# Another issue order in a fused attention and expert kernel: squares are copied behind their masks, first outputs stand behind last copies

## The chip, the core and the metric

The kernel runs on one core of one Trainium2 chip. The metric is the device time of one launch in microseconds (us). The engines are named as in the profile: PE (TensorE), PEld (its weight loads), ACT (ScalarE), DVE (VectorE), POOL (GpSimd) and SP (SyncE, which issues most transfers). PSUM, the memory that PE writes, has eight banks here; ACT and DVE copy results out of it.

## What is computed

Three stages follow each other. The first is a linear attention with a complex decay, for 4 batches, 8 heads, 768 positions and a head dimension of 48:

```python
for t in range(S):
    new_re = ar * S_re - ai * S_im
    new_im = ar * S_im + ai * S_re
    S_re, S_im = new_re + k[t] (outer) v[t], new_im
    y[t] = q[t] @ S_re            # per batch and head
```

Its output, 3072 rows of 384, goes to eight experts (each row to one, by the largest gate, if `x @ w_skip > 0`): `out = x + gate * relu(x @ w1[e]) @ w2[e]`. The last stage is `max(x @ w1, x @ w2, x @ w3) @ w_out`.

## The kernel before

The kernel is one program in which a planner, the class `Plan`, writes down all operations with engine, estimated duration, what they read and write, and a bias; `order()` then plays them through with these estimates and issues the instructions in the order in which they start there. Each engine works through its own list in that order, and the program adds a semaphore wait wherever an instruction touches something that an earlier one, in the issue order, still uses. For a PSUM bank these waits are between any two engines that use the bank, readers included: where ACT's copy out of a bank is issued ahead of DVE's reading of it, DVE waits for ACT, and the other way round. The planner of before does not know all of these waits: its keys name parts of a bank.

A level orders what is ready on an engine: earlier operations first, shifted by the bias, which comes from the table `PRIO` (one number for each kind of operation and unit of work). On PE the planner adds `TURN = 95` ns where the tiling form of the matmuls changes (whole array, 128 rows by 64 columns, 64 by 64), and prefers an operation of the current form over others unless its level is more than `KEEP` behind.

The attention has two parts that run beside each other. The **front end** takes five units of work (batches 0, 1 and 2, and batch 3 in two pieces). On ACT (L443) and DVE (L475, L513, L559) it works out magnitudes, phases and running products of the decay from `wa`, `wCD`, `wR` and scales q and k (`wqk`); each unit needs two sets of ACT functions, so two table loads (L378). Transfers on SP (L570) then stack the result into `qks`. The **steps** are 48: 6 chunks of 128 positions for two halves of the heads and 4 batches. One step consists of

- L607 (PE, whole array): a transposition of k into a `pk` bank, copied by ACT at L609 to `kn`;
- L620 (PE): products of k and q, "squares", into one of two `pp` banks (bank_109 and bank_110). DVE multiplies four of the six by a mask at L623, and ACT copies the other two at L626, both into `pt`, of which there are two;
- L636 (PE): the running state in banks 113 and 114, copied by ACT at L641 to `st`;
- L651 (PE), not for the first chunk: the "first output", q times the state, into one of two `py` banks (bank_111 and bank_112);
- L658 (PE, 64 by 64): the squares times v and `cross`, added to the same columns of the same `py` bank; ACT copies the sum at L661 to `ysb`;
- L665 (PE): `ysb` times `w9p` into other columns (`px`) of the same bank; ACT takes these out with the "last copies", L673 to `xt` and L675 to `lgw`.

The step after the next uses the same `py` bank, so its L651 (or L658, in a first chunk) meets the last copies there. Behind the attention come the experts and the last stage, whose operations are all recorded at L49. Their first operations are mixed into the last steps.

Of the kernel before, what the change touches and what calls it, by code (L numbers as in the profile page):

```python
# [58 lines left out]
class Plan:  # L59
# [6 lines left out]
    BASE = ()  # L66
    YIELD = None
    TURN = 95
    KEEP = 10

    def __init__(self, flat=None):

# [63 lines left out]
    def order(self):  # L136
# [21 lines left out]
        while done < n:  # L158
# [4 lines left out]
            for e, q in ready.items():  # L163
                if q and free[e] <= now:
                    k = 0
                    if e == "PE":
                        k = min(range(len(q)), key=lambda k: q[k][0] + (self.form.get(q[k][1], 0) != last) * self.KEEP)
                    i = q[k][1]
# [35 lines left out]
    def issue(self):  # L204
        for i in self.order():
# [37 lines left out]
MERGE = dict(ratio=(1, 1, 1, 1, 3), log=(1, 1, 1, 2, 3), size=(1, 1, 1, 1, 1), inv=(1, 1, 1, 1, 1),  # L243
             newton=(1, 1, 1, 2, 1), angle=(1, 1, 1, 2, 2), turn=(1, 1, 1, 1, 2), trig=(1, 1, 1, 1, 3))
LATE = 1
PRIO = dict(FE=(-30, 400, 400, 100, 60), FT=(250, 400, 100, 300, 10), AE=(300, 60, 0, 150, 0), AT=(-200, 250, 10, 30, 0),
            scale=(0, 200, 10, -30, -30), fin=(60, 200, 200, 250, 30), kn=(250, -100, -30, -150), free=(-150, 400, 0, 250),
            mask=(200, 300, 250, 0), z=(-60, 60, -100, 60), ysb=(-200, 200, -100, -150), xt=(-150, -150, -150, -150))
NXT = 2
NCD = 3  # L250
NQK = 3
# [49 lines left out]
def attention(tc, ctx, pl, a4, qk4, v, vx, w9, x_dram, lg, ident, phend, rhoend, keep, banks, swap, shift):  # L301
# [61 lines left out]
    mask = const.tile([P, HC], F32, name="mask")  # L363
# [66 lines left out]
    def load_cross(b, c):  # L430

        if (b, c // VG) not in crosses:
            t, k = crosses[b, c // VG] = pl.take("cross")
            cols = slice(c // VG * VG * VW, (c // VG + 1) * VG * VW)
            pl.dma(lambda: nc.sync.dma_start(out=t[:, :VG * VW], in_=vx[b][:, cols]), 5 * P * VG * VW, (), (k,),
                   after=stacked.get(b - 1, ()))
        return crosses[b, c // VG]
# [3 lines left out]
    def A_(f, out, in_, **kw):  # L441
        act(t_act(out[0].free_size()) + (94 if not isinstance(kw.get("bias", 0.0), float) else 0),
            lambda: nc.scalar.activation(out=out[0], in_=in_[0], func=f, **kw), keys(in_), keys(out))  # L443
# [3 lines left out]
    def many(us, nm):  # L447

        if len(us) == 1:
            return T[us[0], nm]  # L450
        (tag, h), (b, g, c0, c1) = tags[nm], us[0]
        k, cf = homes[tag, b, g][1:]
        return wide[tag][:, k[1]:k[1] + len(us), h, C * (c0 - cf):C * (c1 - cf)], keys(*(T[u, nm] for u in us))
# [14 lines left out]
    def keys(*ts):  # L468
        return sum((t[1] for t in ts), ())

    def V_(name, out, *ins, n=None, bias=0, **kw):
        fn = getattr(nc.vector, name)
        t = (t_dcp if name == "tensor_scalar" else t_dve)(out[0].free_size() if n is None else n)
        names = ("in0", "in1")[:len(ins)]
        pl.add("DVE", t, lambda: fn(out=out[0], **{m: i[0] for m, i in zip(names, ins)}, **kw),  # L475
               keys(*ins), keys(out), bias=bias)
# [4 lines left out]
    def ratio(us):  # L481
# [4 lines left out]
        for w in runs(us, "a", "ratio"):  # L486
            A = many(w, "ar")
            A_(AF.Ln, many(w, "C"), A, scale=1.0 - TINY)
            A_(AF.Exp, many(w, "D"), many(w, "C"), scale=-1.0 - TINY)
            V_("tensor_tensor", many(w, "ai"), many(w, "D"), many(w, "ai"), op=ALU.mult, bias=PRIO["FE"][now[0]])  # L490

    def stage_e(us):
# [5 lines left out]
        for w in runs(us, "CD", "size"):  # L498
            Ct = many(w, "C")
            V_("scalar_tensor_tensor", Ct, many(w, "ar"), Ct, scalar=1.0 / 0.999, op0=ALU.mult, op1=ALU.max, bias=PRIO["FE"][now[0]])  # L500
            for u in w:
# [6 lines left out]
    def decay(u):  # L508
# [3 lines left out]
        def scan():  # L512
            nc.vector.tensor_tensor_scan(out=Dt[0], data0=Dt[0], data1=Ct[0],  # L513
                                         initial=rhoend[:, i:i + 1] if c0 else INV0, op0=ALU.mult, op1=ALU.mult)
        pl.add("DVE", t_scan(n), scan, keys(Ct, Dt) + (("rho", i),), keys(Dt), bias=PRIO["FE"][now[0]])
        pl.add("DVE", 75, lambda: nc.vector.tensor_copy(out=rhoend[:, i:i + 1], in_=Dt[0][:, n - 1:n]), keys(Dt), (("rho", i),),  # L516
               bias=PRIO["FE"][now[0]])

    def scale(us):
# [3 lines left out]
        for w in runs(us, "CD", "newton"):  # L523
            R0, Ct, Dt = many(w, "R0"), many(w, "C"), many(w, "D")
            V_("scalar_tensor_tensor", R0, Dt, Ct, scalar=-1.0, op0=ALU.mult, op1=ALU.mult, bias=PRIO["scale"][now[0]])
            V_("scalar_tensor_tensor", Ct, R0, Ct, scalar=2.0, op0=ALU.add, op1=ALU.mult, bias=PRIO["scale"][now[0]])
            for u in w:
# [48 lines left out]
    def qkeys(b, h, c):  # L576
        i = (2 * b + h // 4) % NST
        return tuple(("qks", i, h % 4, ri, e, c) for ri in range(2) for e in range(0, D, 16))
# [3 lines left out]
    def step(b, hh, c):  # L582
# [3 lines left out]
        hk = sum((qkeys(b, 4 * hh + h, c) for h in range(4)), (("blank", i),))  # L586
        vt, vk = T[b, "v"]
# [3 lines left out]
        xv, xk = load_cross(b, c)  # L591
# [9 lines left out]
        if not last:  # L601
            pk, pkk = pl.take("pk")
            kn, knk = pl.take("kn")
# [9 lines left out]
        pt, ptk = pl.take("pt")  # L613

        free = ("free", ptk)
        p6, t6 = six(pp), six(pt)

        def f():
            for j, n, o in heads:
# [3 lines left out]
        masked = pl.add("DVE", t_dve(4 * HC) + 10, lambda: nc.vector.tensor_tensor(  # L623
            out=t6[:, 0:4], in0=p6[:, 0:4], in1=mask[:, None, :].to_broadcast([P, 4, HC]), op=ALU.mult), (ppk,), (ptk,),
            bias=PRIO["mask"][b])
        pl.add("ACT", t_acp(2 * HC), lambda: nc.scalar.copy(pt[:, 4 * HC:6 * HC], pp[:, 4 * HC:6 * HC]), (ppk,), (free,),  # L626
               bias=PRIO["free"][b])
        sp = prev.get((b, hh)) if c else None
        if not last:
            z = zst[hh][:, 0:4 * ZW]  # L630
# [13 lines left out]
        py, pyk = pl.take("py")  # L644
        px = py[:, XO:XO + 2 * XW].rearrange("p (j w) -> p j w", j=2)
        py = py[:, 0:2 * C].rearrange("p (j t) -> p j t", j=2)
        ysb, ysk = pl.take("ysb")
# [3 lines left out]
                nc.tensor.matmul(py[side[h % 2], h // 2, :], sp[0][:, h * D:h * D + 64], Q[:, h, sl], start=h < 2, stop=False,  # L651
                                 skip_group_check=True)
        if c:
            pl.add("PE", 4 * 109, f, hk + (sp[1], ("px", pyk)), (pyk,), form=1)

        def f():
            for j, n, o in heads:
                nc.tensor.matmul(py[side[o], j, n * HC:], half(j, n, o), t6[side[o], quads(j, n), :],  # L658
                                 start=c == 0 and j + n == 0, stop=n == 1, skip_group_check=True)
        pl.tail = masked, pl.add("PE", 4 * 165, f, (vk, xk, ptk, free), (pyk,), form=2)  # L660
        pl.add("ACT", t_acp(256), lambda: nc.scalar.copy(ysb, py), (pyk,), (ysk,), bias=PRIO["ysb"][b])  # L661
        def f():
            for j in range(2):
# [5 lines left out]
        xt, xtk = xts[b, c]  # L669
# [20 lines left out]
    def steps(us):  # L690
        for b, g, c0, c1 in us:
            if (b, "v") not in T:
                load_v(b)
            done[b, g] = c1
        new = []
        for k, (b, hh) in enumerate((b, hh) for b in range(B) for hh in range(2)):
            c1 = min(done.get((b, g), 0) for g in (hh, hh + 1))
            c0 = stepped.get((b, hh), 0)
            new += [(c - c0, k, b, hh, c) for c in range(c0, c1)]
            stepped[b, hh] = c1  # L700
        for _, _, b, hh, c in sorted(new):
            step(b, hh, c)
# [1078 lines left out]
```

## Time and profile before

| | us |
|---|---|
| median of 3 runs | 681.35 (677.01 to 682.12) |
| profiled execution, its own time | 681.32 |
| profiled execution, span of its instructions | 679.6 |
| PE busy | 597.0 (88% of the span) |
| PEld busy | 550.7 (81%) |
| DVE busy | 457.3 (67%) |
| ACT busy | 384.6 (57%) |

The profiled execution is one run on the chip. An engine is busy while one of its instructions runs; for PE this is an upper reading, since matmuls overlap and their ends are modelled. Idle time is put down to the instruction whose semaphore came last. The shares are means over stages of very different make: PE does nothing before about 52 us, works on the steps until about 234 us, and then on the experts and the last stage.

### The profile page before, as it was taken

Reading aid. Unit: us, or ns where it says so; the run is one execution under the profiler, and the core shown is the slowest. Engines: PE = TensorE matmul, PEld = TensorE weight load, DVE = VectorE, ACT = ScalarE, POOL = GpSimd, SP = SyncE. Lnnn points to the kernel's source line nnn. Section 1 sums busy time; section 2 is a strip of 40 time slices with the busy share of each in tenths; the row PEclk is TensorE's granted clock in tenths of the full one; section 3 lists DMA queues with packets and bytes.
Section 4 is the critical chain, followed back from the end, with each engine's and each line's share of the span. In section 5 each row is a group of like instructions: output and inputs, shape, how many; then the busy total and the mean of one; then the engine's idle time right before and its main releaser. Section 6 shows DMA issues by size and latency. Waiting matters only on the chain.

```text
span 679.6 us, 14174 instructions
## 1 busy us (share of the span) xinstructions
PE 597.0 (88%) x5669; PEld 550.7 (81%) x5669; DVE 457.3 (67%) x748; ACT 384.6 (57%) x800; POOL 64.5 (9%) x73
## 2 busy tenths in 40 slices
PE   0008789979999999989999998999999999999996
PEld 0007678968888889979999997889899898998996
DVE  5998978969778775999999954845547365303120
ACT  7798979889875755776676532432324333213121
POOL 1000000000003130030200143404011000000000
PEclk9999999989999999999999999999999999999999
DMA  9979769797658767887786366315043050010000
GB/s 306 296 186 257 284 176 303 250 264 254 177 165 239 249 200 240 276 273 264 261 270 218 117 186 210 117 68 182 30 152 105 1 197 13 12 36 0 25 25 28
DMA packets 60025, 117.40 MB, mean 173 GB/s; under 512 B 6032, under 2 KB 45472, under 8 KB 59952
## 3 DMA queue, kind: packets, MB, share of 16 engines
q1 hardware_dynamic: 51584, 84.57, 40.1%
q10 hardware_dynamic: 4512, 19.66, 8.2%
q0 software_dynamic: 3856, 12.19, 6.1%
q8 instruction: 46, 0.75, 0.5%
q14 instruction: 27, 0.22, 0.1%
HBM read 82.59 MB, written 12.58 MB: 140 GB/s over the span
## 4 chain that ended last, share of the span: by engine, by line
PE 68%; ACT 10%; DVE 9%; DMA 7%; issue 3%; SPq 1%; POOL 0%; ACTq 0%; POOLq 0%; DVEq 0%
PE bank L49 56%; PE bank L658 3%; PE bank L620 3%; ACT wCD L443 3%; ACT wa L443 3%; PE bank L651 2%; DMA qks<-wqk 2%; PE bank L636 2%; PE bank L665 2%; DVE wqk L475 1%; DMA wraw<-y_slot,r_grow 1%; DVE u L49 1%; DMA wqk<-in_qk 1%; DMA x<-in_m 1%; DVE wa L559 1%
## 5 line engine op out<-in xcount | busy, mean ns | idle before, releaser
L49 PE MATMUL bank<-ar,wh 128*128 128x512 f32 (+1 forms) x504 | 137.1, 360 | 0.1
L49 PEld LDWEIGHTS bank<-ar,wh 128*128 128x128 f32 x504 | 90.0, 189 | 14.1 <-DVE xs L49 0.3
L49 PE MATMUL bank<-ar,wl 128*128 128x512 f32 (+1 forms) x252 | 90.6, 360 | 0.0
L49 DVE TENSOR_TENSOR xs<-bank,xs 128x512 f32<-128x512 f32 (+1 forms) x42 | 25.8, 614 | 69.3 <-PE bank L49 69.2
L607 PE MATMUL bank<-ident,qks 96*128 96x96 f32 x160 | 23.2, 272 | 52.3 <-DMA qks<-wqk 52.3
L49 PE MATMUL bank<-ar,sm 128*128 128x384 f32 x348 | 67.0, 338 | 0.0
L49 PE MATMUL bank<-xth,ar 128*128 128x256 f32 x312 | 63.5, 288 | 3.0 <-DVE sm L49 2.1
L607 PEld LDWEIGHTS bank<-ident,qks 96*128 96x128 f32 x160 | 15.7, 147 | 55.6 <-issue 46.7
L49 PEld LDWEIGHTS bank<-ar,sm 128*128 128x128 f32 x348 | 59.2, 189 | 0.0
L49 DVE TENSOR_TENSOR ar<-wraw,ar 128x768 fp32r<-128x768 f32 x58 | 54.7, 953 | 4.8 <-ACT ar L49 4.5
L49 PEld LDWEIGHTS bank<-xth,ar 128*128 128x128 f32 x312 | 50.9, 190 | 5.0 <-DVE sm L49 3.4
L49 PE MATMUL bank<-woh,sm 128*128 128x384 f32 x192 | 53.9, 334 | 0.0
L49 ACT CAST ar<-wraw 128x768 fp32r<-128x768 f32 x58 | 48.1, 835 | 9.8 <-PE bank L49 8.6
L49 PEld LDWEIGHTS bank<-ar,wl 128*128 128x128 f32 x252 | 47.6, 189 | 7.1
L49 ACT COPY ysb<-bank 128x384 f32<-128x384 f32 x40 | 18.4, 478 | 60.8 <-PE bank L49 60.6
L443 ACT ACTIVATE wCD<-wCD 128x768 f32<-128x768 f32 (+3 forms) x67 | 51.4, 785 | 2.3 <-DVE wCD L513 2.1
L658 PE MATMUL bank<-pt,v 64*64 64x64 f32 (+1 forms) x384 | 42.3, 253 | 3.2 <-ACT xt L673 1.4
L620 PE MATMUL bank<-qks 128*64 128x128 f32 (+1 forms) x768 | 44.1, 260 | 0.7 <-DVE rhoend L516 0.5
L49 PE MATMUL bank<-xtl,ar 128*128 128x256 f32 x156 | 44.0, 282 | 0.0
L49 ACT ACTIVATE wraw<-wraw 128x768 f32<-128x768 f32 x24 | 19.6, 842 | 42.4 <-DVE u L49 36.6
L658 PEld LDWEIGHTS bank<-pt,v 64*64 64x64 f32 x384 | 36.2, 136 | 8.8 <-ACT xt L673 2.6
L443 ACT ACTIVATE wa<-wa 128x768 f32<-128x768 int32 (+8 forms) x53 | 40.9, 792 | 3.8 <-DVE wa L559 3.2
(223 smaller groups left out, 1422.1 us busy)
## 6 DMA issues: line engine op xcount, KB each, us to landing
wraw<-in_w SPq DMA_DIRECT2D x62, 384.0 KB, 4.5
wraw<-in_a ACTq DMA_DIRECT2D x12, 768.0 KB, 5.2
wqk<-in_qk SPq DMA_DIRECT2D x9, 768.0 KB, 10.0
x<-in_m ACTq DMA_DIRECT2D x9, 768.0 KB, 6.3
qks<-wR SPq DMA_DIRECT2D x18, 288.0 KB, 4.6
qks<-wqk SPq DMA_DIRECT2D x18, 288.0 KB, 5.6
v<-in_v SPq DMA_DIRECT2D x4, 1152.0 KB, 13.1
wa<-in_a SPq DMA_DIRECT2D x6, 768.0 KB, 13.7
```

Source lines behind the costliest of these rows:

```text
L49: return lambda *a, **kw: fn(*map(placed, a), **{n: placed(x) for n, x in kw.items()})
L443: lambda: nc.scalar.activation(out=out[0], in_=in_[0], func=f, **kw), keys(in_), keys(out))
L475: pl.add("DVE", t, lambda: fn(out=out[0], **{m: i[0] for m, i in zip(names, ins)}, **kw), keys(*ins), keys(out), bias=bias)
L559: nc.vector.tensor_tensor_scan(out=Bt[0], data0=A[0], data1=zero1.to_broadcast([P, n]), initial=phend[:, i, c0 - 1:c0] if c0 else 0.0, op0 ...
L607: nc.tensor.transpose(pk[:, h, :2 * D], K[:2 * D, h, sl], ident[:2 * D, :2 * D])
L620: nc.tensor.matmul(p6[side[o], quads(j, n), :], K[:, 2 * j + o, part[n]], Q[:, 2 * j + o, part[n].start:sl.stop], start=True, stop=True)
L636: nc.tensor.matmul(z[side[o], h * ZW:h * ZW + ZW], kn[:, at:at + HC], vcols(h, ZW), start=c == 0 and h == 0, stop=c == NC - 2 and h == 3, ...
L651: nc.tensor.matmul(py[side[h % 2], h // 2, :], sp[0][:, h * D:h * D + 64], Q[:, h, sl], start=h < 2, stop=False, skip_group_check=True)
L658: nc.tensor.matmul(py[side[o], j, n * HC:], half(j, n, o), t6[side[o], quads(j, n), :], start=c == 0 and j + n == 0, stop=n == 1, skip_gro ...
L665: nc.tensor.matmul(px[side[o], j, :], ysb[:, j, side[o]], w9p[:, 2 * hh + j, :], start=True, stop=True)
```

## The change

Four edits, all in what the planner knows; no instruction's work is changed. In the changed program the lines behind the table of numbers stand one lower (L620 is L621, and so on).

```diff
-    KEEP = 10
+    KEEP = 30
...
-            mask=(200, 300, 250, 0), z=(-60, 60, -100, 60), ysb=(-200, 200, -100, -150), xt=(-150, -150, -150, -150))
+            free=(100, 30, 60, 150), mask=(-30, 30, 60, -60), z=(-30, -200, -60, -30), ysb=(-100, 0, -60, -150),
+            xt=(-150, 250, 200, 200))
...
         pl.add("ACT", t_acp(2 * HC), lambda: nc.scalar.copy(pt[:, 4 * HC:6 * HC], pp[:, 4 * HC:6 * HC]), (ppk,), (free,),
-               bias=PRIO["free"][b])
+               after=(masked,), bias=PRIO["free"][b])
...
         if c:
-            pl.add("PE", 4 * 109, f, hk + (sp[1], ("px", pyk)), (pyk,), form=1)
+            pl.add("PE", 4 * 109, f, hk + (sp[1],), (pyk, ("px", pyk)), form=1)
...
-        pl.tail = masked, pl.add("PE", 4 * 165, f, (vk, xk, ptk, free), (pyk,), form=2)
+        pl.tail = masked, pl.add("PE", 4 * 165, f, (vk, xk, ptk, free), (pyk, ("px", pyk)), form=2)
```

The first `pl.add` is ACT's copy at L626, which now stands behind DVE's mask of the same bank. The other two are L651 and L658: by writing the key of `px` they now stand behind the last copies that read it (L673, L675). All other numbers of `PRIO` for the attention change too; the two lines stand for them. `KEEP` triples the weight of an unchanged form.

In the order of instructions the three longest lists keep their heads and their tails: up to the first steps, and from the last steps on, every engine's rows are the same as before, and POOL's are the same throughout. In between they are permuted. Three places follow.

PE's list, second and third step of the program (bank_111 and bank_112 are the `py` banks, bank_109 and bank_110 the `pp` banks, bank_113 and bank_114 the states). Before:

```order
L620 MATMUL bank_109<-qks_128 64x2x64 x2
L620 MATMUL bank_109<-qks_128 64x64 x2
L620 MATMUL bank_109<-qks_128 64x2x64 x2
L620 MATMUL bank_109<-qks_128 64x64 x2
L665 MATMUL bank_111<-w9p,ysb_162 64x105 x4
L651 MATMUL bank_111<-qks_128,st_148 64x128 x4
L636 MATMUL bank_113<-v_140,kn_156 64x64 x8
L620 MATMUL bank_110<-qks_129 64x2x64 x2
```

The first output into bank_111 stands directly behind L665 into the same bank. The same place now:

```order
L666 MATMUL bank_111<-w9p,ysb_162 64x105 x4
L621 MATMUL bank_110<-qks_129 64x2x64 x2
L621 MATMUL bank_110<-qks_129 64x64 x2
L621 MATMUL bank_110<-qks_129 64x2x64 x2
L621 MATMUL bank_110<-qks_129 64x64 x2
L637 MATMUL bank_114<-v_140,kn_157 64x64 x8
L621 MATMUL bank_109<-qks_128 64x2x64 x2
L621 MATMUL bank_109<-qks_128 64x64 x2
L621 MATMUL bank_109<-qks_128 64x2x64 x2
L621 MATMUL bank_109<-qks_128 64x64 x2
L652 MATMUL bank_111<-qks_128,st_148 64x128 x4
```

Two groups of squares and one of the state now stand between L665 and the first output into its bank.

ACT's list in the second function set of the second unit (L443 on `wa` is the front end, the others are copies of the steps). Before:

```order
L675 COPY lgw<-bank_111 128x18
L443 ACTIVATE wa<-wa 128x768 x2
L609 COPY kn_157<-bank_108 128x384
L443 ACTIVATE wa<-wa,halfpi 128x768
L443 ACTIVATE wa<-wa 128x768 x3
L443 ACTIVATE wa<-wa,halfpi 128x768
L443 ACTIVATE wa<-wa 128x768 x2
L443 ACTIVATE wa<-wa,halfpi 128x768
L641 COPY st_150<-bank_114 96x192
```

Eight operations of the front end stand between a copy of k and a copy of the state. Now:

```order
L444 ACTIVATE wa<-wa 128x768
L642 COPY st_150<-bank_114 96x192
L610 COPY kn_157<-bank_108 128x384
L444 ACTIVATE wa<-wa 128x768
L627 COPY pt_161<-bank_110 128x128
L444 ACTIVATE wa<-wa,halfpi 128x768
L627 COPY pt_160<-bank_109 128x128
L610 COPY kn_157<-bank_108 128x384
L662 COPY ysb_163<-bank_112 128x256
L444 ACTIVATE wa<-wa 128x768 x2
```

The copies now stand between the operations of the front end, and at most four of these follow each other anywhere.

ACT's list at the first squares, with what each row waits for. Before:

```order
L609 COPY kn_156<-bank_107 128x384 [waits PE_49]
L626 COPY pt_160<-bank_109 128x128 [waits PE_49]
L443 ACTIVATE wCD<-wCD 128x768 [waits DVE_49]
L641 COPY st_148<-bank_113 96x192 [waits PE_49]
L609 COPY kn_156<-bank_107 128x384 [waits PE_49,Activation_49]
```

ACT's copy of the first squares stood ahead of DVE's mask and waited for PE. Now:

```order
L642 COPY st_149<-bank_113 96x192 [waits PE_49]
L610 COPY kn_156<-bank_107 128x384 [waits Activation_49]
L627 COPY pt_160<-bank_109 128x128 [waits DVE_49]
L444 ACTIVATE wCD<-wCD 128x768 [waits Activation_49]
L444 ACTIVATE wCD<-wCD 128x768 [waits DVE_49]
```

The copy waits for DVE's mask and stands two copies later.

## Rows read from the trace of the kernel before

**Rows 1.** Busy time by stretch (us from the span's start; columns as its second line says).

```profile
core 0 of [0], span 679.6 us
core 0: us, PE busy (x) PEld busy (x) DVE busy (x) ACT busy (x) POOL busy (x), PEclk, DMA share, GB/s
...
57.00:204.00 147.00, 132.01 (x2468) 118.33 (x2468) 121.08 (x169) 130.17 (x329) 0.00 (x0) 0.98 0.77 236
204.00:234.00 30.00, 29.19 (x560) 25.86 (x562) 24.30 (x55) 20.98 (x62) 8.41 (x12) 1.00 0.84 258
57.00:234.00 177.00, 161.20 (x3028) 144.19 (x3030) 145.38 (x223) 151.15 (x390) 8.41 (x12) 0.98 0.78 240
...
324.00:665.00 341.00, 337.82 (x1946) 313.96 (x1945) 187.65 (x316) 128.59 (x236) 39.87 (x31) 1.00 0.33 110
```

**Rows 2.** Groups by line, 57 to 234 us: busy us, mean ns | idle before, releasers.

```profile
...
L658 PE MATMUL bank<-pt,v 64*64 64x64 f32 (+1 forms) x384 | 42.3, 253 | 3.2 <-ACT xt L673 1.4 <-DVE pt L623 0.9 <-ACT pt L626 0.4
...
L636 PE MATMUL bank<-v,kn 128*64 128x64 f32 x624 | 26.5, 229 | 5.5 <-ACT st L641 3.6 <-ACT kn L609 1.7
...
L665 PE MATMUL bank<-w9p,ysb 128*64 128x105 f32 x380 | 26.0, 263 | 3.6 <-ACT ysb L661 3.6
...
L651 PE MATMUL bank<-qks,st 128*64 128x128 f32 x320 | 24.7, 277 | 2.5 <-ACT lgw L675 1.8 <-ACT xt L673 0.6
...
L607 PE MATMUL bank<-ident,qks 96*128 96x96 f32 x152 | 21.0, 266 | 0.4 <-DMA qks<-wqk 0.4
...
L623 DVE TENSOR_TENSOR pt<-bank,mask 128x256 f32<-128x256 f32 x48 | 19.9, 419 | 19.4 <-PE bank L620 10.2 <-ACT pt L626 8.6
...
L673 ACT COPY xt<-bank 128x192 f32<-128x192 f32 x47 | 15.2, 330 | 6.4 <-PE bank L651 3.4 <-PE bank L665 2.0 <-PE bank L658 0.7
...
L626 ACT COPY pt<-bank 128x128 f32<-128x128 f32 x47 | 12.6, 274 | 5.7 <-DVE pt L623 2.6 <-PE bank L620 2.6
...
```

**Rows 3.** Groups by line and shape, 0 to 330 us, two lines.

```profile
...
L475 DVE TENSOR_TENSOR wqk<-wqk,wa 128x1536 f32<-128x1536 f32 x9 | 15.8, 1755 | 0.3
...
L675 ACT COPY lgw<-bank 128x18 f32<-128x18 f32 x48 | 9.0, 190 | 7.7 <-PE bank L658 5.6 <-PE bank L651 2.1
...
```

**Rows 4.** Waits, 57 to 234 us: total us, times, longest us.

```profile
...
PE bank L665 <- ACT ysb L661: 3.6, 4, 1.9
...
ACT pt L626 <- DVE pt L623: 2.6, 7, 0.6
...
```

**Rows 5.** Timeline of ACT: start us, us, engine line operation.

```profile
...
76.12 0.97 ACT L443 ACTIVATE wa<-wa,halfpi 128x768 f32<-128x768 f32 x1
76.96 2.47 ACT L443 ACTIVATE wa<-wa 128x768 f32<-128x768 int32 x3
...
82.60 0.29 ACT L641 COPY st<-bank 96x192 f32<-96x192 f32 x1
...
```

**Rows 6.** Timeline of PE at 82.95 us.

```profile
...
82.95 1.12 PE L636 MATMUL bank<-v,kn 128*64 128x64 f32 x16 [3.19 <-ACT st L641]
...
```

**Rows 7.** The chain of waits, two groups of squares (start us, us, what).

```profile
...
84.07 1.28 PE bank L620 x16
...
94.39 0.67 PE bank L620 x16
...
```

**Rows 8.** PE's busy time in stretches of 4 us, with the granted clock.

```profile
...
76.00:80.00 4.00, 3.52 (x68) 1.00 0.75 276
80.00:84.00 4.00, 1.05 (x18) 0.80 0.18 46
...
```

**Rows 9.** Timelines of ACT and of PE at 145 to 147 us.

```profile
...
145.19 0.17 ACT L675 COPY lgw<-bank 128x18 f32<-128x18 f32 x1 [1.01 <-PE bank L658]
...
147.02 0.83 PE L665 MATMUL bank<-w9p,ysb 128*64 128x105 f32 x8 [1.90 <-ACT ysb L661]
...
```

**Rows 10.** Timeline at 96 us: the last product of L658, then L636.

```profile
...
96.02 0.22 PE L658 MATMUL bank<-pt,cross 64*64 64x64 f32 x1
...
96.17 0.69 PE L636 MATMUL bank<-v,kn 128*64 128x64 f32 x16
...
```

More of the change, by code (lines that the diff above doesn't have):

```diff
@@ L245 @@
 LATE = 1
-PRIO = dict(FE=(-30, 400, 400, 100, 60), FT=(250, 400, 100, 300, 10), AE=(300, 60, 0, 150, 0), AT=(-200, 250, 10, 30, 0),
-            scale=(0, 200, 10, -30, -30), fin=(60, 200, 200, 250, 30), kn=(250, -100, -30, -150), free=(-150, 400, 0, 250),
-            mask=(200, 300, 250, 0), z=(-60, 60, -100, 60), ysb=(-200, 200, -100, -150), xt=(-150, -150, -150, -150))
+PRIO = dict(FE=(-150, 400, 200, -200, 400), FT=(400, 400, 100, 10, 200), AE=(10, -100, 60, 150, -200),
+            AT=(-60, -30, -150, -100, 0), scale=(-100, 0, -30, -30, -150), fin=(10, 0, 400, 10, 30), kn=(-30, 200, 250, -150),
+            free=(100, 30, 60, 150), mask=(-30, 30, 60, -60), z=(-30, -200, -60, -30), ysb=(-100, 0, -60, -150),
+            xt=(-150, 250, 200, 200))
 NXT = 2
```

## The prediction

> **What bounds the kernel now.** I read the busy time by stretch first. The span is 679.6 us, and 1.7 us lie around it (681.32 in all for this execution, as good as the median of 681.35). From 324 to 665 us PE is busy for 337.8 of 341 us [rows 1]; nothing is to be had there, and the change moves nothing there. The permuted part of the lists lies between about 57 and 234 us, 177 us long. There no engine is full: PE is busy for 161.2 us, ACT for 151.2, DVE for 145.4 [rows 1]. So PE is idle for 15.8 us, ACT for 25.9 and DVE for 31.6.
>
> Next, what the idle time waits for [rows 2]. PE's is nearly all spent behind ACT's copies: L636 behind L641 and L609 (3.6 and 1.7), L665 behind L661 (3.6), L651 behind the last copies (1.8 and 0.6), L658 behind the last copies, the mask and the squares (1.4, 0.9, 0.4). Only 0.4 us is spent behind the stacked data of the front end (L607). PE therefore always has steps to do, and what holds it is how soon ACT gives back a bank or a tile. ACT in its turn stands idle behind PE in a way that the steps don't ask for: L675 waits 5.6 us for L658 and 2.1 for L651, L673 waits 3.4 for L651 and 0.7 for L658 [rows 2, 3]. These are next steps' products into the bank that the copies have yet to read, issued ahead of them: 11.8 us of ACT. The squares do the same between ACT and DVE: the mask waits 8.6 us for L626, and L626 2.6 us for the mask [rows 2].
>
> From 204 to 234 us PE is at 29.2 of 30 us [rows 1], working off steps whose data lie ready. A microsecond that PE gains earlier moves this end forward, and with it the experts, whose lists are unchanged.
>
> **The change part by part.** I counted in both orders.
>
> *The long run on ACT.* Before, eight front-end operations follow each other between copies; now the longest run is four (twice), and most stand alone. In the trace the run is the stretch from 76.12 to 82.60 us, and the copy of the state comes at its end [rows 5]. PE waits 3.19 us for it, and then its groups are slow: the state group takes 1.12 us where another takes 0.69 at 96.17, the squares 1.28 where others take 0.67 [rows 6, 7, 10]. In the rows the granted clock is 1.00 from 76 to 80 us and 0.80 on average from 80 to 84, that is, PE fell from 2.4 to 1.2 GHz while it waited [rows 8]. The whole is worth 3.2 + 0.43 + 0.61 = 4.2 us at most. It is nothing if the front end sets the end, since the run's 6.5 us are still to be done. L607's 0.4 us speaks against that, ACT's 130.2 of 147 us until 204 us [rows 1] for it. I take 3.0.
>
> *First outputs behind last copies.* Before, in 19 of the 46 cases where a `py` bank is used again, at most one group of PE stood between L665 and the next product into the bank (12 times none); now 5 (once none). L675 waits for PE in 14 of 48 places in the order before and in 3 now. PE's own waits of this kind are 1.8 + 0.6 + 1.4 = 3.8 us; I scale by 14/19 and take 2.8, between 0 (the copies are needed all the same) and 3.8. ACT's 11.8 us come back to PE only through a later copy. The plainest case: L675 waits 1.01 us for L658 at 145.19, the `ysb` copy behind it is late, and PE waits 1.90 us for that at 147.02 [rows 9]. I take 1.0 for this one and nothing for the rest; all of it would be 11.8.
>
> *Squares behind masks.* Squares are now written two steps ahead more often: in 30 of 46 cases they stand ahead of the L658 that frees their `pt`, 4 before, and at least three groups lie between squares and the L658 that uses them (one before). PE's waits of 0.9 + 0.4 = 1.3 us should go; I take all of it. The price is ACT's: all 48 copies wait for DVE now, 23 before. Seven such waits cost 2.6 us [rows 4]; in proportion to the count they become 5.4, so 2.8 more, of which I charge half, 1.4, since ACT is idle for 25.9 us anyway. The bounds are 0 and 25 times the mean wait of 0.37, 9.3 us.
>
> *Fewer changes of form.* PE's list has 139 changes of tiling form before and 124 now. At such a change the next start comes 0.15 us after the last one (96.02 to 96.17) [rows 10], and within a group of squares a start comes every 0.67/16 = 0.04 us [rows 7]: 0.11 each, 15 of them 1.6 us. The Trainium skill ("TensorEngine Tiling (Array Packing)", Key Properties) says that changing the tiling mode drains the engine; an estimate by that is the whole last product, 0.22 us each and 3.3 us in all. The trace does not show so much: the new group starts before that product's modelled end. I stay with 1.6.
>
> *What gets tighter.* L665 now stands closer behind its L658: in 10 of 48 cases there is at most one group to cover the `ysb` copy, 3 before. Four waits of this kind cost 3.6 us, 0.9 each [rows 4]; seven more would be 6.3. One group hides about half of such a wait, so I charge 0.4 each, 2.8 us. Behind the late L665 come its own last copies and, with them, the bank.
>
> Transfers: SP's list has the same ones, moved by a few places, and PE does not wait for them; their cover is the backlog of steps. DVE's 1.755 us products [rows 3] stand directly ahead of a mask in 12 places, 8 before; what waits there is L626, counted above.
>
> The sum: 3.0 + 2.8 + 1.0 + 1.3 + 1.6 - 1.4 - 2.8 = 5.5 us, so 681.3 - 5.5 = 675.8 us.
>
> **The rivals.** *More than that.* The planner now sees the waits that the chip sees, so that copies arrive when PE wants them throughout. If half of PE's 15.8 us goes, with the 1.0 us of slow groups and the 1.6 us of form changes, it is 7.9 + 2.6 = 10.5 us: 671 us. For it: ACT's 11.8 us are three quarters of PE's idle time. Against it: the bank is still one, and the copies still have to be made between two products.
>
> *No gain, the wait only changes places.* The turns on a bank remain. If the front end's work on ACT sets the end, the long run gives nothing and the one case at 147 us returns elsewhere: 2.8 + 1.3 + 1.6 - 1.4 - 2.8 = 1.5 us, 680 us. For it: ahead of the last front-end operation ACT makes 222 copies now and 220 before, so steps and front end end as close together as they did.
>
> *Slower: ACT stands behind DVE.* DVE's list has products of 1.755 us [rows 3], and a mask behind one holds L626 and with it every copy behind L626. If each of the 25 new waits costs the mean of 0.37 us and the four additional masks behind long products 1.755 each, it is 9.3 + 7.0 = 16.3 us on ACT; with ACT the engine that PE waits for, half of that on PE is 8.2, put in the place of the 1.4, so that the sum turns to 5.5 + 1.4 - 8.2 = -1.3. All of it gives 6.9 - 16.3 = -9.4 us, 690.7; I put this case between, at 687. It decides from a new wait of 6.9/25 = 0.28 us on each copy. The Trainium skill ("TensorE: Matmul & The Clock Gate", Architectural detail: the array is 16x 32x32, not 1x 128x128) states that the queues of ScalarE and VectorE are strictly first in, first out; by that rule nothing behind a held L626 can pass it, which is this rival. The trace agrees: after each wait of L626 ACT goes on with the next row of its list. Against it: with squares two steps ahead a mask has three groups or more of time, and before only 7 of the 23 copies that stood behind a mask waited visibly.
>
> **How the numbers follow.** The forecast of about 5.5 us has 0.45 (671 to 680 by its bounds), more than that 0.22, no gain 0.22, slower 0.11. A measurement of this kernel can tell about 1% (6.8 us) from no change: faster means under 674.5, slower over 688.2. Of the forecast's 0.45, 0.17 lies under 674.5; with nearly all of the first rival (0.21) that is 0.38 for faster. Slower has most of the last rival and nothing else: 0.09, rounded up to 0.12 for what its bounds leave. The rest, 0.50, is within 1%. The range leaves out the far ends of the first and the last rival: 668 to 685 us.
>
> **What would show it.** In the changed profile the waits of L675 and L673 for L651 and L658 (11.8 us) should be nearly gone, and the mask's wait for L626 (8.6 us) gone. L626's wait for the mask should stand near 5 us, L665's for L661 near 6. PE should have no wait of 3 us and no fall of the clock near 80 us. PE's idle time between 57 us and the end of the steps should be about 11 us, and the last L665 should come about 5.5 us before its 234 us. The prediction is wrong if L626's waits exceed 10 us, if L607 waits for the stacked data (then the front end is late), or if a gain at the end of the steps is given back before 324 us.

## The result, and the profile after

The changed kernel takes 671.65 us (median, 670.54 to 673.07), the kernel before 680.86 (median of four runs each): a ratio of 0.9875, 95% interval 0.9831 to 0.9919. The forecast was 675.8 us, so the direction was right and the gain of 9.2 us larger than the 5.5 of the sum. The profiled execution of the changed kernel took 670.54 us, its span is 668.8, and against the 681.32 us of the profiled execution before it is 10.8 us shorter.

The busy time by stretch (columns as in [rows 1]), from 57 us to the end of the last L666, the line that was L665. That end is 224.46 us now (the stretch shown stops 0.03 us short of it) and was 234.43, so the steps end 10.0 us earlier; before, PE was busy for 161.6 of those 177.4 us.

```profile
57.00:224.43 167.43, 156.74 (x3032) 140.39 (x3031) 144.09 (x221) 148.89 (x392) 7.80 (x12) 1.00 0.82 253
324.00:665.00 341.00, 336.00 (x1926) 312.08 (x1924) 178.30 (x302) 123.80 (x227) 35.82 (x29) 1.00 0.32 105
```

PE's busy time fell from 161.6 to 156.7 us and its idle time from 15.8 to 10.7. In a second profile of the changed kernel (a_again below) they are 158.3 and 10.5, so two executions of one order differ by 1.6 us in the busy time. From the end of the steps to the end of the span it is 445.2 us before and 444.3 after: nothing is given back behind the steps. PE's waits in the stretch (total us, times, longest us), all of 0.8 us or more in total:

```profile
PE bank L637 <- ACT kn L610: 1.8, 3, 0.8
PE bank L621 <- ACT pt L627: 1.8, 3, 0.9
PE bank L652 <- ACT lgw L676: 1.4, 3, 0.5
PE bank L666 <- ACT ysb L662: 1.4, 5, 0.4
PE bank L621 <- DMA qks<-wqk: 1.4, 1, 1.4
PE bank L608 <- ACT kn L610: 0.9, 2, 0.6
PE bank L637 <- ACT st L642: 0.9, 1, 0.9
PE bank L652 <- ACT xt L674: 0.8, 1, 0.8
```

No single wait is longer than 1.4 us, where before there were one of 3.19 and one of 1.90 [rows 6, 9]. ACT's largest waits in the same stretch, and the mask's on DVE, are these:

```profile
ACT ysb L662 <- PE bank L659: 6.3, 6, 2.3
ACT pt L627 <- DVE pt L624: 4.9, 5, 1.7
DVE pt L624 <- PE bank L659: 6.9, 7, 3.4
DVE pt L624 <- PE bank L621: 4.5, 6, 1.3
```

The mask waits for PE alone now, no more for ACT's copy (8.6 us before [rows 2]). L676 and L674 wait no more for the next products into their bank (11.8 us before [rows 2]). ACT now stands idle where the data are not yet made: the `ysb` copy waits for the newest L659.

The clock, in slices of 4 us (length, PE busy, granted clock, DMA share, GB/s). First three slices of the kernel before, which [rows 8] does not have; then the same places after:

```profile
84.00:88.00 4.00, 3.58 (x58) 0.78 1.00 264
144.00:148.00 4.00, 1.95 (x30) 0.90 1.02 267
148.00:152.00 4.00, 3.95 (x58) 0.67 1.04 263
```

```profile
80.00:84.00 4.00, 4.00 (x90) 1.00 0.50 152
84.00:88.00 4.00, 3.28 (x68) 1.00 0.97 261
144.00:148.00 4.00, 3.99 (x76) 1.00 1.03 284
148.00:152.00 4.00, 3.79 (x80) 1.00 0.97 246
```

A slice of 0.78 means that PE had the lower of its two levels, 1.2 GHz, for 0.22 / 0.5 of the 4 us. Summed over the four slices below 1.00 this is 6.8 us before; after, no slice between 52 us and the end of the steps is below 1.00. ACT's copies near 80 us now stand between front-end operations:

```profile
80.48 0.40 ACT L662 COPY ysb<-bank 128x256 f32<-128x256 f32 x1
80.73 0.89 ACT L444 ACTIVATE wa<-wa 128x768 f32<-128x768 int32 x1
81.48 0.35 ACT L642 COPY st<-bank 96x192 f32<-96x192 f32 x1
81.68 0.90 ACT L444 ACTIVATE wa<-wa 128x768 f32<-128x768 int32 x1
82.42 0.30 ACT L627 COPY pt<-bank 128x128 f32<-128x128 f32 x1
```

### The profile page after: what moved, and what is told of

It is laid out like the page before. It is cut to its first block, busy times and chain, and to the rows that moved or that the text cites. A ratio compares the mean times of both kernels' runs of the same rounds, so it can differ in the third digit from the quotient of the medians.

```text
span 668.8 us, 14161 instructions
## 1 busy us (share of the span) xinstructions
PE 592.6 (89%) x5669; PEld 547.0 (82%) x5669; DVE 455.7 (68%) x748; ACT 383.0 (57%) x800; POOL 62.9 (9%) x73
## 4 chain that ended last, share of the span: by engine, by line
PE 65%; DVE 11%; ACT 11%; DMA 6%; issue 4%; SPq 1%; POOL 0%; ACTq 0%; POOLq 0%; DVEq 0%
PE bank L49 56%; ACT wCD L444 4%; DVE wqk L476 2%; PE bank L659 2%; PE bank L621 2%; DVE wR L476 2%; ACT wa L444 2%; DVE u L49 2%; PE bank L637 1%; DMA w9p<-in_w 1%; DMA wraw<-y_slot,r_grow 1%; PE bank L666 1%; PE bank L652 1%; DMA x<-in_m 1%; ACT kn L610 1%
## 5 line engine op out<-in xcount | busy, mean ns | idle before, releaser
L608 PE MATMUL bank<-ident,qks 96*128 96x96 f32 x160 | 22.8, 269 | 52.3 <-DMA qks<-wqk 50.8
L608 PEld LDWEIGHTS bank<-ident,qks 96*128 96x128 f32 x160 | 15.5, 147 | 56.0 <-issue 45.4
L621 PE MATMUL bank<-qks 128*64 128x128 f32 (+1 forms) x768 | 42.4, 254 | 3.2 <-ACT pt L627 1.8
L621 PEld LDWEIGHTS bank<-qks 128*64 128x64 f32 x768 | 38.5, 141 | 5.3 <-ACT pt L627 2.5
L49 PE MATMUL bank<-lnh,ar 128*128 128x384 f32 x144 | 40.9, 337 | 0.0
```

Source lines behind the costliest of these rows:

```text
L49: return lambda *a, **kw: fn(*map(placed, a), **{n: placed(x) for n, x in kw.items()})
L608: nc.tensor.transpose(pk[:, h, :2 * D], K[:2 * D, h, sl], ident[:2 * D, :2 * D])
L621: nc.tensor.matmul(p6[side[o], quads(j, n), :], K[:, 2 * j + o, part[n]], Q[:, 2 * j + o, part[n].start:sl.stop], start=True, stop=True)
```

## Experiments

Single executions of one kernel differ by up to 10 us here (the kernel before took 679.4 to 689.6 us in 31 runs of the first series), so the ratios rest on medians, and a profile shows where one execution, named beside it, lost its time. All readings of the 14 profiles, up to the end of the steps (the end of the last L665 or L666; PE idle and the longest single wait from 57 us; "low" is the time at 1.2 GHz, summed over slices as above):

| kernel | ratio to before | profiled us | steps end | PE idle | longest wait | low |
|---|---|---|---|---|---|---|
| before | 1 | 681.32 | 234.43 | 15.8 | 3.19 | 6.8 |
| after | 0.9875 | 670.54 | 224.46 | 10.7 | 1.36 | 0 |
| a_again | 0.9867 | 675.34 | 225.82 | 10.5 | 0.88 | 0 |
| e_keep | 1.0056 | 691.42 | 242.70 | 22.1 | 3.40 | 20.4 |
| e_know | 1.0047 | 685.34 | 237.65 | 17.0 | 4.91 | 10.3 |
| e_prio | 1.0045 | 686.77 | 236.57 | 16.8 | 2.69 | 10.2 |
| e_nokeep | 1.0002 | 683.36 | 234.57 | 16.3 | 5.26 | 6.8 |
| e_noprio | 1.0034 | 687.99 | 238.02 | 19.2 | 6.16 | 13.6 |
| e_noknow | 1.0018 | 684.36 | 236.06 | 17.4 | 4.34 | 13.8 |
| e_spread | 1.0007 | 682.50 | 234.03 | 15.1 | 3.40 | 13.7 |
| e_fill | 0.9990 | 683.98 | 232.55 | 13.9 | 1.90 | 3.4 |
| e_stall | 1.0016 | 684.84 | 234.83 | 18.8 | 8.65 | 10.2 |
| e_mend | 0.9999 | 687.93 | 231.99 | 13.9 | 4.24 | 10.2 |
| e_np_run | 0.9963 | 682.91 | 232.52 | 12.3 | 3.27 | 6.9 |

### The parts alone, and the whole without one part

The first four kernels take `KEEP` alone, the three edges alone, the table alone, and everything but `KEEP`. Of e_keep:

```diff
-    KEEP = 10
+    KEEP = 30
```

Of e_know (the same new key stands behind L658's):

```diff
-               bias=PRIO["free"][b])
+               after=(masked,), bias=PRIO["free"][b])
...
-            pl.add("PE", 4 * 109, f, hk + (sp[1], ("px", pyk)), (pyk,), form=1)
+            pl.add("PE", 4 * 109, f, hk + (sp[1],), (pyk, ("px", pyk)), form=1)
```

Of e_prio, which has the whole new table, the first line of it:

```diff
-PRIO = dict(FE=(-30, 400, 400, 100, 60), FT=(250, 400, 100, 300, 10), AE=(300, 60, 0, 150, 0), AT=(-200, 250, 10, 30, 0),
+PRIO = dict(FE=(-150, 400, 200, -200, 400), FT=(400, 400, 100, 10, 200), AE=(10, -100, 60, 150, -200),
```

e_nokeep has the last two together.

Expected of e_keep: 

> The kernel before with KEEP = 30 alone. Its order has 117 changes of tiling form on PE (139 before, 124 after the whole change), squares two steps ahead in 27 of 46 cases (4 and 30), but L675 behind PE in 14 places and a run of eight front-end operations on ACT, as before. Terms theory (each edit is worth its own term): 22 changes of form at 0.11 us are 2.4 us and PE's 1.3 us behind masks and squares go, about 677; the fall of the clock near 80 us stays. Theory that the knowledge of the turns does all: 681, as before. Theory that the sticky form does most: 673 or less.

Expected of e_know: 

> The kernel before with the two edges alone (copies of squares behind masks, first outputs behind last copies), old numbers, KEEP = 10. L675 stands behind PE in 1 place (14 before), at most one group between L665 and the next product into its bank in 5 of 46 cases (19), but 155 changes of form (139) and squares ahead in 10 of 46. Terms theory: 2.8 + 1.0 + 1.3 for the waits, less 16 changes of form at 0.11 = 1.8, about 677.5. Theory that the knowledge does all: 672. Theory that the numbers were fitted to the old edges and must be refitted: 681 or more.

Expected of e_prio: 

> The kernel before with the new table of numbers alone. Longest run of front-end operations five (eight before, four after), 134 changes of form, L675 behind PE in 9 places. Terms theory: the long run gives 3.0 and five changes of form 0.6, about 677, and no fall of the clock at 80 us. Theory that the numbers are good only with the edges for which they were made: 681 or more.

Expected of e_nokeep: 

> The whole change but with KEEP = 10. 156 changes of form (124 with KEEP = 30), squares two steps ahead in 8 of 46 cases (30), the edges' counts as after the change. Terms theory: 32 changes of form at 0.11 us are 3.5 us more than the whole change (671.7), 675. Theory that the edges and the numbers do all: 672. Theory that the sticky form, through the squares that run ahead, does most: 678 or more.

Measured: 1.0056 [1.0028, 1.0084], 1.0047 [1.0016, 1.0079], 1.0045 [1.0015, 1.0075] and 1.0002 [0.9979, 1.0024]. None of the three parts gains anything by itself; each costs 3 to 4 us. The idea that each part carries a term of the sum fell. What the profiles have in common are single long waits of PE and falls of the clock: 4.91 us in e_know and 3.40 in e_keep at the long run near 80 us (eight operations in e_keep, six in e_know), another of 3.11 in e_keep at 151 us, 2.69 in e_prio at 100 us, 5.26 in e_nokeep at 133 us. In e_prio the two do not belong together: no slice near the 2.69 us wait is below 1.00, and the clock falls from 144 us on, where waits of 1.74, 1.00, 0.83 and 0.75 us follow each other.

```profile
103.09 0.32 PE L659 MATMUL bank<-pt,v 64*64 64x128 f32 x1 [2.69 <-ACT pt L627]
```

```profile
104.00:108.00 4.00, 2.75 (x49) 1.00 1.02 283
148.00:152.00 4.00, 2.45 (x20) 0.50 1.06 281
```

DVE, PE and the clock in e_nokeep at 133 us:

```profile
133.59 1.75 DVE L476 TENSOR_TENSOR wR<-wqk,wa 128x1536 f32<-128x1536 f32 x1
135.45 1.76 DVE L476 TENSOR_TENSOR wqk<-wqk,wa 128x1536 f32<-128x1536 f32 x1
137.12 0.75 DVE L624 TENSOR_TENSOR pt<-bank,mask 128x256 f32<-128x256 f32 x2
```

```profile
132.29 0.69 PE L637 MATMUL bank<-v,kn 128*64 128x64 f32 x16 [0.71 <-ACT kn L610]
138.23 0.47 PE L659 MATMUL bank<-pt,v 64*64 64x128 f32 x1 [5.26 <-ACT pt L627]
```

```profile
136.00:140.00 4.00, 1.77 (x22) 0.50 1.01 220
140.00:144.00 4.00, 4.00 (x70) 0.73 0.17 48
```

Six of DVE's long products stand in a row from 126.5 to 137.1 us, the masks behind them, the `pt` copies behind the masks (and behind five front-end operations on ACT), and PE stands for 5.26 us. It is near the rival "slower: ACT stands behind DVE", but ACT shows no wait for DVE here: its own five operations end at about the same time as the masks, and the first `pt` copy follows at 137.93 us. The Trainium skill ("TensorE: Matmul & The Clock Gate", Architectural detail: the array is 16x 32x32, not 1x 128x128) has the queues of ScalarE and VectorE strictly first in, first out; the trace agrees, since masks and copies go out only behind the runs, at 137.12 us and later.

The next series has the whole change once more, and the whole without the table and without the edges.

Expected of a_again: 

> The whole change once more, on the chip of the next three runs. Both theories expect what was measured: 0.983 to 0.992 of the time before, no granted clock under 1.00 between 57 us and the end of the steps, PE idle there near 11 us, the end of the steps near 224 us.

Expected of e_noprio: 

> KEEP = 30 and the three edges, with the old table of numbers. Theory A, the parts add up: edges and KEEP measured +3.2 and +3.8 us alone, so +7 us, ratio 1.010. Theory B, the time is PE's work plus one or two single long waits that each order happens to hold, each with a fall of the granted clock behind it: the order statistics are the best of all (three places instead of 19 with a first output close behind L665, squares ahead in 34 of 46), but the table was not made for this order, so at least one PE wait of over 2 us, a clock under 1.00 in some 4 us window, ratio 0.995 to 1.008.

Expected of e_noknow: 

> KEEP = 30 and the new table, without the three edges. Theory A (sum of the parts): KEEP +3.8 and table +3.1, so +7 us, ratio 1.010. Theory B: the edges decide where the last copies and the masks stand, and without them the new table gives another order with long waits: 0.997 to 1.010, with a PE wait of over 2 us and a fall of the clock. A third theory, that the edges are worth nothing beside table and KEEP: as the whole change, 0.983 to 0.992.

Measured: 0.9867 [0.981, 0.9923], 1.0034 [1.0007, 1.0061] and 1.0018 [0.9991, 1.0045]. The gain of the whole change came again in another series of runs. Each pair of parts is as slow as before or slower: the sum of the parts would have given 1.010 for both, the third theory of e_noknow 0.987. Of these six incomplete versions none gains. With KEEP and edges but the old table, the run of eight on ACT is still there, and PE pays twice as much for it as before:

```profile
83.07 1.12 PE L651 MATMUL bank<-qks,st 128*64 128x128 f32 x8 [6.16 <-ACT lgw L675]
...
231.77 1.97 PE L651 MATMUL bank<-qks,st 128*64 128x128 f32 x16 [3.19 <-ACT lgw L675]
```

Here the first output, which the edge puts behind the last copies, is the instruction that stands: the copies it waits for are behind the run.

### One wait put in, one wait mended

In the next kernels the planner's order is kept and a few operations are issued elsewhere or several times. The edit has this form in all of them, with other numbers of operations:

```diff
     def issue(self):
-        for i in self.order():
-            if self.ops[i][2] is not None:
-                self.ops[i][2]()
+        seq = self.order()
+        for i, j in self.MOVE.items():
+            seq.remove(i)
+            seq.insert(seq.index(j), i)
+        for i in seq:
+            for _ in range(self.REPEAT.get(i, 1)):
+                if self.ops[i][2] is not None:
+                    self.ops[i][2]()
```

It adds eight lines ahead of the steps: L644 of e_fill is L636 of before, L645 of e_stall is L637 of after.

**e_stall** is the changed kernel with `REPEAT = {217: 25}`, the copy of one state written 25 times.

Expected: 

> The whole change with one addition: the copy of one state near 74 us is written 25 times instead of once, some 4.8 us more on ACT with the state product of the next step behind it. If a single long wait costs its length and the clock, PE waits 3 to 4.5 us there, the clock falls behind it, and the time rises by 4.5 to 6.5 us, ratio 0.990 to 0.996 to before (0.987 for the whole change). If such a delay is made good by the steps that lie ready (ACT is idle for 18 us of the stretch), the end of the steps moves by under 1.5 us, ratio 0.986 to 0.989.

ACT and PE of e_stall, and its clock:

```profile
75.02 8.64 ACT L650 COPY st<-bank 96x192 f32<-96x192 f32 x25
```

```profile
84.09 1.12 PE L645 MATMUL bank<-v,kn 128*64 128x64 f32 x16 [8.65 <-ACT kn L618]
```

```profile
80.00:84.00 4.00, 0.00 (x0) 0.50 0.00 0
84.00:88.00 4.00, 3.91 (x42) 0.50 0.00 0
```

Measured 1.0016 [0.9994, 1.0037]. The copies took longer than I had reckoned, so the wait is 8.65 us and not 3 to 4.5. What it costs is the answer: against the whole change the ratio rises by 0.0145 (the mean of 0.9875 and 0.9867 taken), 9.9 us of 684, and the steps end 9.0 to 10.4 us later. Next to nothing of the wait was made good in the 150 us of steps behind it; from 84 to 88 us PE ran its 3.91 us at half speed besides, which is about 2 us of work lost. One stall undoes the whole change.

But the added copies hold up all that stands behind them on ACT, the front end's operations too. The front end's last table load comes at these times, in the kernel before, the changed kernel, e_stall and e_nokeep:

```profile
192.90 1.28 ACT L378 ACT_TABLE_LOAD   x1
183.12 1.28 ACT L379 ACT_TABLE_LOAD   x1
193.83 1.28 ACT L387 ACT_TABLE_LOAD   x1
186.37 1.28 ACT L379 ACT_TABLE_LOAD   x1
```

In the changed kernel the front end is 9.8 us earlier than before, and in e_stall all of that is gone again. So e_stall does not tell PE's wait from a late front end. An early front end is not enough by itself: in e_nokeep it is 6.5 us earlier than before, and the steps end no earlier (234.57 us).

**e_fill** is the kernel before with `REPEAT = {269: 6}`, the transposition ahead of the 3.19 us wait written six times.

Expected: 

> The kernel before with one addition: PE's transposition ahead of the 3.2 us wait near 80 us is written six times instead of once (into the same bank, before its copy), some 2.4 us of PE work that lies inside the wait. If the slow groups behind the wait come from the clock that fell because PE stood still, PE's wait shrinks to about 0.8 us, no 4 us window from 80 to 88 us is under 1.00 (0.80 and 0.78 before), the groups behind it take 0.69 and 0.67 to 0.89 us instead of 1.12 and 1.28, and the end of the steps moves forward by 1 to 1.5 us; ratio 0.997 to 1.000. If repeated transpositions do not keep the clock, or the slow groups have another cause, nothing but the wait's name changes.

PE in e_fill, and its clock:

```profile
78.96 2.20 PE L615 MATMUL bank<-ident,qks 96*128 96x96 f32 x24
82.63 0.69 PE L644 MATMUL bank<-v,kn 128*64 128x64 f32 x16 [1.47 <-ACT st L649]
83.14 0.84 PE L628 MATMUL bank<-qks 128*64 128x128 f32 x16
```

```profile
80.00:84.00 4.00, 2.53 (x52) 1.00 0.24 66
84.00:88.00 4.00, 2.80 (x52) 1.00 0.99 253
```

The clock stays, and the state group takes 0.69 us instead of 1.12 [rows 6], the squares 0.84, where the timeline of before has 1.50. Useful work goes on at the same moment (0.3 us earlier in this execution); by the L665 of 147.02 us [rows 9], which is at 145.39 here, the gain is 1.63. So the clock alone was worth 1.3 us at this place by these two executions, and the steps end 1.9 us earlier. The Trainium skill ("TensorE: Matmul & The Clock Gate", Part 1: The HAM clock gate (the "warmup" mystery)) says that the clock is set by how busy the engine has been of late; the two slices agree, since the same wait of the state group, filled, leaves it at 1.00. The time, 0.999 [0.9957, 1.0024], is too coarse to show it, and this execution lost it again behind the steps, where PE waited 2.46 us for DVE at 303 us and the clock was at 0.66 from 304 to 308.

**e_spread** is the kernel before with five copies issued inside the run of eight: `MOVE = {217: 379, 190: 395, 207: 395, 215: 396, 230: 396}`.

Expected: 

> The kernel before with its order, except that five copies of ACT (one of the state, two of ysb, two of pt), which stood behind the eight front-end operations at 76 to 83 us, are issued between them. Theory B, a single long wait costs its length and the clock: PE's wait of 3.2 us near 80 us and the clock of 0.80 and 0.78 behind it go, the end of the steps moves from 234.4 to about 230 us, and the time falls by 4 to 5 us, ratio 0.993 to 0.995. The rival, that the wait only changes places since the front end's work on ACT is the same: the end of the steps moves by under 1.5 us, ratio 0.998 to 1.000.

PE in e_spread:

```profile
80.33 0.90 PE L673 MATMUL bank<-w9p,ysb 128*64 128x105 f32 x16
81.06 0.60 PE L659 MATMUL bank<-qks,st 128*64 128x128 f32 x8
85.06 0.47 PE L666 MATMUL bank<-pt,v 64*64 64x128 f32 x1 [3.40 <-ACT xt L681]
```

Measured 1.0007 [0.9983, 1.0031]; the steps end 0.4 us earlier. PE now does 2.6 us of work at 79 to 82 us, and then stands for 3.40 us behind the last copies, which follow on ACT behind the rest of the run, a table load and a copy of k. The rival holds: the wait changed places.

**e_mend** is e_nokeep with the masks, the copies to `pt`, two L659 and the copies to `ysb` issued ahead of the runs at 132 us.

```diff
+    MOVE = {554: 681, 567: 691, 555: 690, 568: 710, 559: 905, 572: 905, 560: 906, 573: 909}
```

Expected: 

> The whole change but KEEP = 10 (measured at 1.000), with its order mended by hand at one place: two masks are issued ahead of the long DVE products at 130 to 137 us, and two copies to pt, two first sums of PE and two copies to ysb ahead of the run of front-end operations on ACT there. If that order lost its gain to the one wait of 5.3 us and the clock behind it (0.50 from 136 to 140 us), PE's wait there falls under 2 us, the end of the steps moves from 234.6 to about 229 us, and the ratio is 0.990 to 0.994. If the wait changes places, as with the five copies moved in the kernel before, ratio 0.997 to 1.001.

PE in e_mend:

```profile
144.56 1.12 PE L660 MATMUL bank<-qks,st 128*64 128x128 f32 x8 [4.24 <-ACT lgw L684]
```

Measured 0.9999 [0.9975, 1.0022]. The 5.26 us wait is gone and one of 4.24 us for the last copies ends 6 us later, again with the clock at 0.50: they stand behind seven front-end operations in a row on ACT. The steps end 2.6 us earlier. (The profiled execution is the slowest of ten, so its loss behind the steps says nothing of the median.)

**e_np_run** is e_noprio with one number of the new table, the one that decides the run of eight (of the line, only the entry that differs):

```diff
-    AT=(-200, 250, 10, 30, 0)
+    AT=(-200, -30, 10, 30, 0)
```

Expected: 

> KEEP = 30 and the three edges with the old table, in which one number is the new one: AT of the second unit -30 instead of 250, the bias that puts the front end's second function set ahead of the copies. If the run of eight on ACT and its wait of 6.2 us at 77 to 83 us came of that number and the wait is worth its length and the clock, the time falls from 687.6 by 6 to 9 us, ratio 0.990 to 0.995. If the order made new holds another long wait (its longest run is six), ratio 0.998 to 1.006.

PE in e_np_run, and its clock:

```profile
143.94 0.65 PE L620 MATMUL bank<-qks 128*64 128x128 f32 x8 [3.27 <-DMA qks<-wqk]
```

```profile
148.00:152.00 4.00, 4.00 (x50) 0.50 0.97 272
```

Measured 0.9963 [0.9936, 0.9989], 4.9 us under e_noprio and the only one of these versions whose whole interval lies below the time before; I had expected 6 to 9 us, or nothing. The run's wait is gone (no wait over 0.9 us near 80 us), but PE waits 3.27 us for the stacked data at 144 us. These data are not later than elsewhere: the two transfers that PE waits for (`qks<-wqk`) are issued from 138.42 us on, in e_noprio from 139.08, before from 139.57. PE comes to them sooner, and then the front end holds it. In the changed kernel they are issued from 132.51 us on: there the front end is ahead as well. The transfers in e_np_run and in the changed kernel:

```profile
138.42 2.14 SPq L570 DMA_DIRECT2D qks<-wqk  x2
132.51 1.14 SPq L571 DMA_DIRECT2D qks<-wqk  x2
```

## Why the forecast was right in direction and short in size

**What was as told.** L674's and L676's waits for the next products are gone (11.8 us before), and the mask's wait for the copy (8.6). The copy's wait for the mask is 4.9 us, forecast "near 5". PE is idle for 10.7 us in the stretch, forecast 11 (more on that below). No wait of 3 us and no fall of the clock is left near 80 us. Nothing is given back behind the steps. One sign of being wrong came in part: L608 does not wait for the stacked data, but L621 does, once, for 1.4 us (0.6 in a_again).

**The term for L665 had the wrong sign.** I charged 2.8 us for an L665 closer to its L658, from a mean of 0.9 us for each such wait [rows 4], and gave only 1.0 to the copies no longer held by L675. There are five such waits now, 1.4 us in all, the longest 0.4, where there were 3.6. The 0.9 was not a price of closeness alone: ahead of the 1.90 us wait, more than half of the 3.6, L675 held ACT for 1.01 us [rows 9], a cause that the change removes. Instead of -1.8 for the two terms together it is +2.2.

**The clock was booked at one place of two.** The slow groups near 80 us stood in the sum with at most 1.0 us; e_fill shows 1.3 there. The 1.90 us wait at 147 us was read as a wait alone, and the slice behind it (0.67 from 148 to 152 us) not at all. PE's busy time fell by 4.9 us, of which the fewer changes of form were forecast to bring 1.6; no run measured those by themselves. An estimate from the rows gives the clock 3.0 us: the 1.3 of e_fill, and for 144 to 152 us, where two slices (0.90 and 0.67) hold 3.4 us at 1.2 GHz, half of that, 1.7. The rest, 1.9 us, is not certain, since a_again has 1.6 us more busy time than the first profile of the changed kernel.

**The other terms.** By PE's waits the long run brought 2.8 (L637's 5.5 to 2.7) where 3.0 was booked with its slow groups, the last copies 1.6 (3.8 to 2.2) and not 2.8. The squares' 1.3 us went, but L621 waits 1.8 for its `pt` copies, so they brought -0.5 and not -0.1. New are 1.4 us for stacked data and 0.9 for a copy of k; some 1.8 us of small waits went.

**What was luck.** The end of the steps moved by 10.0 us, 5.1 of idle and 4.9 of busy time. That the idle time came out near 11 us is luck: without the changes of form the sum has 3.9 us, which would have left about 12, and its terms missed on both sides, L665 and the copies held by it by 4.0 us one way, the last copies, the squares and the two new waits by 3.9 the other. What the sum missed is the busy time: it had 1.6 us for the changes of form and at most 1.0 for slow groups.

**What the sum could not say.** Each term was read as a gain that its part would bring, and no part brings one. The rival "more than that" gave 671 us, near what was measured, with a reason near the one the runs support: that copies arrive when PE wants them throughout. The number itself is luck: it took 7.9 us from the idle time, where 5.1 went, and 2.6 from the busy time, where 4.9 went. The runs show why "throughout" matters: in the one execution where a wait was put in, the end moved by more than the wait (e_stall, where the front end was late too), a wait mended at one place stood at the next copy behind the same run (e_spread, e_mend), and every version but the whole change holds a wait of 1.9 us or more, and somewhere before the steps end the clock is down (in e_prio, not behind that wait). Both are missing in the two profiles of the changed kernel, and PE's idle and busy time there account for the whole gain. That it takes a single wait of PE to undo it is not shown, since e_stall holds up the front end with it. Which of the table's numbers removes which wait is open, except for AT of the second unit. It is open, too, why KEEP and the edges need the new table, beyond that the waits of each incomplete order are other ones.

## To carry to other kernels

In a stage where no engine is full, look for the single waits of the engine that sets the end and for what the clock does behind each, rather than adding up means by line: a mean wait is a price of its old cause and must not be charged to a new one. An order that a planner makes from biases is one thing: its numbers belong to its rules, and a part that is tried alone is another order with waits of its own. A copy that is moved out of a run only helps if what the engine needs next is not behind the same run. And an engine that is held less comes sooner to its next limit: in e_np_run that was the front end's data, which the whole change brings earlier too.

## What the runs showed of the hardware

A wait and a fall of the clock do not go together one to one. PE's 1.90 us wait at 147 us was followed by 0.67 in the kernel before, a wait of 1.69 us at 194 us in e_know by 0.64, but one of 2.01 us at 194 us in e_nokeep and one of 2.69 us at 100 us in e_prio by no slice under 1.00. The same copy, written again and again into one tile, comes every 0.35 us (8.64 us for 25 in e_stall), while another copy starts 0.21 us after a copy of a state (73.63 to 73.84 us in the same profile). Whether the engine or a wait that the program adds between copies into one tile makes the difference is not shown.
